# Retention and squared-ReLU feed-forward on one core: every engine's tasks in a new written order, and other places for the long 64x64 runs

## The chip, the cores and the metric

The kernel runs on 1 core of one Trainium2 chip. The metric is device microseconds of one execution; of several runs the median counts. Three runs of the kernel before gave 284.87, 284.90 and 284.92 us.

## The reference

```python
# q, k, v: 8 batches x 8 heads x 576 positions x 64, f32
scores = q @ k.T / sqrt(64)                      # per batch and head
ret    = (scores * gamma_h ** (i - j) for i >= j, else 0) @ v
x      = ret with heads side by side             # 4608 tokens x 512
h      = x @ w_in                                # 512 x 2048
out    = (max(h, 0) ** 2) @ w_out                # 2048 x 512, f32
```

## The kernel before, in words

**Units and groups.** The tokens are cut into 36 units of 128 tokens: 32 "full" ones (one batch, one stretch of 128 positions) and four "tails" that join the last 64 positions of two batches. Two units make a group, so there are 18 groups, g0 to g17. The first eight units (four groups) come in pairs of 256 positions (add_load_pair, add_unit_pair, add_ret_pair); the others one by one (add_load, add_unit, add_ret).

**What a group goes through.** SyncE issues the loads of k, q and v. GpSimd (in the first groups VectorE and ScalarE too) casts them to f16, v times a decay. For the pairs TensorE transposes k and q (task ft, L580) and ScalarE copies the result out (fe, L592); for later units a DMA does it (fx2, L541, tile kqT). Then TensorE computes with 64x64 matmuls, four of which run side by side on the quarters of the array (quad, L501, matmuls at L502): scores, sums of k and v for the running state, and the output of the retention. For the pairs these are the tasks fs, fk, fo1 and fo2. From g4 on one task f0 (L938) emits the output of group g, the scores and the sums of group g+1 in one go: 96 to 128 matmuls of 64x64 in a row, the long 64x64 runs; there are 13 of them. VectorE masks the scores, updates the state and writes x of the group (tile xT: fx at L720 for pairs, L894 for the others; two halves each).

**Feed-forward.** add_ff (L1206) makes eight blocks fb0 to fb7 for a group, each of two tasks j0 and j1 of four matmuls (L1229, tile ph): x times w_in. ScalarE applies the ReLU (fr, L1235) and ScalarE or VectorE the square (fg, L1241, tile gT). For g0 the second product takes 16 tasks fi0 to fi15 for each of its two units s0 and s1 (L1270, tile po): fi0 to fi3 need the first piece of w_out, fi4 to fi7 the second, and so on. From g1 on add_strassen (L1286) does it with seven products of halves of the matrices instead of eight (L1327); this takes sums of gT on VectorE (gS, L1294) and differences of w_out (wT, add_wT, L989, eight tasks i0.h0 to i3.h1 on VectorE). Groups 14 to 16 do the same trick in the first product as well (add_ff1s, L1042).

**Weights.** w_in and w_out come in eight pieces w0 to w7 of 512x512 f32, cast to f16 by the DMA that GpSimd issues (add_weight, L472). w0 to w3 are w_in, w4 to w7 w_out. fb6 and fb7 need w3; wT.i0.h0 and fi0 to fi3 need w4. The load of k for units 4 and 5 waits until w5 has landed (behind, L426).

**What sets the order.** Each piece of work is a task of class Schedule (L78): an engine, a length that the planner assumes, a function that emits its instructions, the tasks that it depends on and the buffers that it takes (eight PSUM banks "ff", load buffers, and so on). emit (L107) plays the tasks forward in time with those lengths. Each time an engine is free, it takes the ready task with the lowest key whose buffers are free; the keys are the 1,828 numbers of PLACES. The order of starts is the order in which the functions are called, and so the order of instructions on every engine, which each engine then follows strictly. 34 tasks "warm" (L411) are matmuls on a zeroed tile, which fill TensorE's first microseconds.

**Places of the runs.** place_runs (L204) goes through TensorE's tasks in order. Ahead of each long run (size over 190 instructions) it takes the next number of PADS and spreads that many no-operations over the small matmul tasks since the run before; sched.filler emits them. PADS moves the run to another place in TensorE's instruction stream and changes nothing else. Before it was

```python
    PADS = (136, 0, 0, 0, 121, 0, 84, 0, 76, 0, 0, 0, 0)      # 417
```

## Time and profile before

| what | value |
|---|---|
| time, median of 3 runs | 284.9 us |
| span of the profiled execution, first to last instruction | 284.5 us |
| what lies around the span (difference of the two) | 0.4 us |
| TensorE matmuls busy | 277.1 us (97%) |
| VectorE, ScalarE, GpSimd busy | 195.8, 190.6, 87.3 us |
| granted TensorE clock | 1.000 |
| moved by DMA | 50.0 MB, mean 176 GB/s |
| TensorE's instructions fetched (instruction queue) | 37 packets, 0.61 MB |

The span counts from the first to the last instruction of the program; all times below are from its start. Busy times of TensorE overstate its work, since matmuls are pipelined: a matmul of 256 columns is listed with 273 ns, but one starts every 109 ns. So the distance from one start to the next is what a matmul costs on TensorE, and every longer distance is a wait or a change of form. By engine "PEld" the profile lists the weight loads, which run beside the matmuls. SP is SyncE's queue.

### The profile page before, as it was taken

The page shows a single profiled execution, that of the slowest core. Times are in us where ns is not written, and L with a number is a line of the kernel's source. Part 1 is how long each engine was busy: PE and PEld are TensorE (multiplying, and loading weights), DVE is VectorE, ACT ScalarE, POOL GpSimd, SP SyncE. Part 2 cuts the span into 40 slices and gives each one's busy share as a digit, 9 for nine tenths or more (in the row PEclk, how much of TensorE's full clock was granted, in tenths as well). Part 3 has the DMA queues.
Part 4 walks back from the last instruction along what each step waited for, and adds up shares of the span by engine and source line. Part 5 has one row for each costly group of instructions (what it writes and reads, how often), then busy time and mean ns, then how long its engine had stood idle before and what let it go on. Part 6 is the DMA issues. An engine that isn't in the chain of part 4 may idle for free.

```text
span 284.5 us, 10916 instructions
## 1 busy us (share of the span) xinstructions
PE 277.1 (97%) x4490; PEld 237.7 (84%) x4490; DVE 195.8 (69%) x371; ACT 190.6 (67%) x360; POOL 87.3 (31%) x123
## 2 busy tenths in 40 slices
PE   8899999999999999899999999999999999999994
PEld 3578767888888888788888888888988999899883
DVE  4783489756867769635859485866986889765742
ACT  5659884678495848566575767577657486668830
POOL 6550035445334346434342523353243200000000
PEclk9999999999999999999999999999999999999999
DMA  7999998999997989999989969999998902020205
GB/s 204 291 207 205 261 313 233 155 241 167 197 189 165 225 193 177 195 241 198 234 196 215 208 163 198 200 146 249 200 168 215 193 0 78 2 76 1 76 0 150
DMA packets 119152, 50.00 MB, mean 176 GB/s; under 512 B 94784, under 2 KB 113728, under 8 KB 119104
## 3 DMA queue, kind: packets, MB, share of 16 engines
q1 hardware_dynamic: 114560, 44.84, 73.4%
q0 software_dynamic: 4224, 4.19, 8.9%
q8 instruction: 37, 0.61, 0.9%
q10 hardware_dynamic: 320, 0.26, 0.3%
q14 instruction: 11, 0.09, 0.1%
HBM read 36.70 MB, written 9.44 MB: 162 GB/s over the span
## 4 chain that ended last, share of the span: by engine, by line
PE 84%; DMA 11%; SPq 3%; POOL 1%; issue 0%; DVE 0%; POOLq 0%
PE po L1327 36%; PE ph L1229 31%; PE ph L1072 7%; DMA w_out<-in_moe_w_out_dram 6%; PE psO L502 4%; DMA pair<-in_v_dram 2%; PE po L1270 2%; PE psc L502 2%; PE psS L502 2%; DMA kqT<-kq 2%; SPq L460 1%; DMA loads<-in_v_dram 1%; SPq L463 1%; PE psT L584 1%; POOL w_out L478 1%; SPq L543 0%
## 5 line engine op out<-in xcount | busy, mean ns | idle before, releaser
L1229 PE MATMUL ph<-xT,w_in 128*128 128x256 f16 x960 | 117.4, 273 | 0.0
L1229 PEld LDWEIGHTS <-w_in 128*128 128x128 f16 x960 | 93.3, 98 | 11.8
L1237 ACT ACTIVATE rl<-ph 128x512 f16<-128x512 f32 x120 | 70.4, 590 | 42.3 <-PE ph L1229 41.7
L1247 ACT ACTIVATE gT<-rl 128x512 f16<-128x512 f16 x101 | 63.4, 630 | 2.7
L1327 PEld LDWEIGHTS <-gS 128*128 128x128 f16 x544 | 51.6, 98 | 6.1
L1327 PE MATMUL po<-wT,gS 128*128 128x256 f16 x408 | 54.9, 273 | 0.0
L1327 PEld LDWEIGHTS <-gT 128*128 128x128 f16 x408 | 39.5, 98 | 4.8
L1300 DVE TENSOR_TENSOR gS<-gT,gS 128x512 f16<-128x512 f16 (+1 forms) x51 | 32.3, 640 | 9.9 <-ACT gT L1247 9.2
L532 POOL TENSOR_TENSOR v<-loads,vdec_full 128x512 f16<-128x512 f32 x24 | 27.2, 1133 | 36.1 <-DMA loads<-in_v_dram 33.0
L1327 PE MATMUL po<-w_out,gT 128*128 128x256 f16 x272 | 37.6, 273 | 0.0
L1300 DVE TENSOR_TENSOR gS<-gT 128x1024 f16<-128x1024 f16 x34 | 25.7, 760 | 11.8 <-ACT gT L1247 9.0
L516 POOL CAST kq<-loads 128x512 f16<-128x512 f32 x32 | 22.1, 692 | 34.7 <-DMA loads<-in_k_dram 26.9
L1350 DVE TENSOR_TENSOR o<-po,u 128x256 f32<-128x256 f32 x33 | 13.9, 422 | 22.7 <-PE po L1327 14.6
L527 POOL CAST kq<-loads 128x512 f16<-128x512 f32 x24 | 16.8, 700 | 31.0 <-DMA loads<-in_q_dram 31.0
L1340 ACT COPY u<-po 128x256 f32<-128x256 f32 x34 | 12.4, 368 | 16.6 <-PE po L1327 16.4
L898 DVE TENSOR_TENSOR xT<-psO,gam_full 128x512 f16<-128x512 f32 x28 | 18.6, 683 | 5.8 <-PE psO L502 5.7
L1327 PE MATMUL po<-wT,gT 128*128 128x256 f16 x136 | 18.8, 273 | 0.0
L1327 PE MATMUL po<-w_out,gS 128*128 128x256 f16 x136 | 18.6, 273 | 0.0
L838 DVE TENSOR_TENSOR rT<-psc,mask_full 128x512 f16<-128x512 f32 x24 | 15.7, 681 | 0.6 <-PE psc L502 0.6
L1106 DVE CUSTOM_DVE_ANT_0 gT<-ph,loads 128x512 f16<-128x512 f32 x18 | 12.1, 685 | 4.2 <-PE ph L1072 3.5
L611 DVE TENSOR_TENSOR R<-stmp,dec 128x512 f16<-128x512 f32 (+1 forms) x18 | 13.5, 750 | 0.4
L1350 DVE TENSOR_TENSOR o<-po,p 128x256 f32<-128x256 f32 x18 | 7.6, 422 | 7.2 <-issue 3.5
(101 smaller groups left out, 310.3 us busy)
## 6 DMA issues: line engine op xcount, KB each, us to landing
out_dram<-o SPq DMA_DIRECT2D x32, 256.0 KB, 2.8
loads<-in_k_dram SPq DMA_DIRECT2D x24, 256.0 KB, 4.6
loads<-in_q_dram SPq DMA_DIRECT2D x96, 64.0 KB, 3.1
loads<-in_v_dram SPq DMA_DIRECT2D x24, 256.0 KB, 3.8
w_in<-in_moe_w_in_dram POOLq DMA_DIRECT2D x4, 512.0 KB, 8.9
w_out<-in_moe_w_out_dram POOLq DMA_DIRECT2D x4, 512.0 KB, 14.4
pair_c<-in_k_dram SPq DMA_DIRECT2D x2, 512.0 KB
pair_c<-in_q_dram SPq DMA_DIRECT2D x4, 256.0 KB
```

The lines of the kernel that those rows point to most:

```text
L502: t = nc.tensor.matmul(out_, lhsT=lhsT, rhs=rhs, start=start, stop=True, skip_group_check=True, tile_position=(64 * row, 64 * col))
L516: op(out=out_.rearrange("p (n b a d) -> p n b a d", n=2, b=2, a=2), in_=in_.rearrange("p (a n b) d -> p n b a d", n=2, a=2))
L527: nc.gpsimd.tensor_copy(out=tile_of["kq", u][:, 1].rearrange("p (t a d) -> p a t d", t=4, a=2), in_=tile_of["q32", u].rearrange("p (a t) d ...
L532: nc.gpsimd.tensor_tensor(out=t, in0=tile_of["v32", u], in1=vdec[kind].rearrange("p (h o) -> p h o", o=1).to_broadcast([P, H, D]), op=ALU. ...
L898: nc.vector.tensor_tensor(out=tile_of["x", g].rearrange("p n (s e i) -> p e (n s) i", s=n, e=2)[:, c], in0=y.rearrange("p (o t r) -> p o r ...
L1072: nc.tensor.matmul(out_[:, e], lhsT=left[:, m, fi * P:(fi + 1) * P], rhs=right()[:, m], start=fresh and e == 0 and m == 0, stop=m == HK - ...
L1229: nc.tensor.matmul(tile_of["ph", g, fb][:, j, :], lhsT=w_in16[:, m, fi * P:(fi + 1) * P], rhs=tile_of["x", g][:, m, :], start=(m == 0), st ...
L1237: nc.scalar.activation(out=t, in_=tile_of["ph", g, fb], func=ACTF.Relu)
L1247: nc.scalar.activation(out=t, in_=rl, func=ACTF.Square)
L1300: (nc.gpsimd if eng == "POOL" else nc.vector).tensor_tensor(out=tile_of["S", g][:, k, sl], in0=in0(sl), in1=in1(sl), op=op)
L1327: nc.tensor.matmul(tile_of["pb", g, bank], lhsT=left(i), rhs=right[:, i, :], start=(start and i == 0), stop=(i == HF - 1), skip_group_chec ...
L1350: nc.vector.tensor_tensor(out=o_tile(u)[:, half * HM:(half + 1) * HM], in0=bank(x), in1=tile_of[name, g], op=ALU.add)
```

## The change

The planner's loop in emit and PLACES are gone. In their place stands ORDER, the numbers of all 1,828 tasks in the order in which they are to be emitted. Tasks, lengths, dependences, buffers and the code that each task emits are the same. 359 of TensorE's 863 tasks, 191 of VectorE's 341, 145 of ScalarE's 354, 77 of SyncE's 170 and 29 of GpSimd's 100 stand at another place of their engine, none of them by more than 26. PADS has other numbers, which add 674 no-operations where there were 417, and they may stand after the 58th task of TensorE (FIRST_PAD), where it was a planned start later than 24.0 us.

```diff
-PLACES = """
-1001794 1001795 1001796 1001797 1001798 1001799 1001800 1001801 1001802 ...
+ORDER = """
+0 34 1 2 3 35 4 5 6 36 7 8 9 70 10 71 11 37 12 76 72 13 73 77 14 38 78 15 ...
...
     def emit(self):
-        assert len(PLACES) == len(self.tasks)
-        for t, x in zip(self.tasks, PLACES):
-            t["key"] = int(x)
-        ready = {e: [] for e in self.LAT}
...
-        assert len(order) == len(self.tasks)
+        order = [self.tasks[int(x)] for x in ORDER]
+        assert len(order) == len(self.tasks) == len(set(ORDER))
+        for t in order:
+            assert t["left"] == 0, t["n"]
+            for w in t["users"]:
+                w["left"] -= 1
         self.place_runs([t for t in order if t["eng"] == "PE"])
         for t in order:
             t["fn"]()
             for i in range(t["pad"]):
                 self.filler()
...
-    PADS = (136, 0, 0, 0, 121, 0, 84, 0, 76, 0, 0, 0, 0)
+    PADS = (121, 55, 15, 0, 38, 23, 79, 3, 67, 71, 147, 55, 0)
+    FIRST_PAD = 58
...
-        for t in tasks:
+        for i, t in enumerate(tasks):
...
-            elif t["size"] <= 8 and t["key"] < 10 ** 6 and t["start"] > 24.0:
+            elif t["size"] <= 8 and i >= self.FIRST_PAD:
                 between.append(t)
```

The two orders around the first pieces of w_out, task by task (numbers are places among TensorE's tasks, counted from 0; the first 58 are the same tasks in both):

```
TensorE  before: 58 g1.fb0.j0  59 g0.fb6.j0  60 g0.fb6.j1  61 g0.fb7.j0  62 g0.fb7.j1  63 g1.fb0.j1  64 g1.fb1.j0  65 g0.fi0.s0
TensorE  after:  58 g0.fi0.s0  59 g0.fb6.j0  60 g1.fb0.j0  61 g1.fb0.j1  62 g0.fb6.j1  63 g0.fb7.j0  64 g0.fb7.j1  65 g0.fi1.s0
VectorE  before: xT g1 first half, xT g1 second half, wT.i0.h0
VectorE  after:  xT g1 first half, wT.i0.h0, xT g1 second half
```

Further on, the transposes of q of units 4 and 5 (ft) stand at place 93 where they stood at 108, and VectorE's cast of v of units 4 and 5 stands ahead of ten tasks (both halves of wT.i1, wT.i2.h1, both halves of wT.i3, three sums gS, a square and a step of the state); in the order before, it stood behind all ten. The long runs f0 of g4, g5, g6 and g7 stand at places 208, 252, 297 and 357, where they stood at 209, 251, 303 and 338; the later ones moved by two places at most. The last 44 tasks of TensorE and the order of the final stores on ScalarE are the same.

## The prediction

> **What bounds the kernel now.** I read the page first, then TensorE's timeline, then what the other engines waited for.

> ```profile
> span 284.5 us, 10916 instructions
> PE 277.1 (97%) x4490; PEld 237.7 (84%) x4490; DVE 195.8 (69%) x371; ACT 190.6 (67%) x360; POOL 87.3 (31%) x123
> DMA   7999998999997989999989969999998902020205
> ```

> TensorE is busy in 97% of the span, and DMA in nine tenths or more of most slices up to about 228 us. TensorE is the bound, with DMA close behind. Going by starts in TensorE's timeline (109 ns from one 256-column matmul to the next), I find almost no gap after 17.4 us. From there to the end only two waits are left: 0.22 us ahead of g0.fi8 (a piece of w_out that landed at 32.50) and 1.3 us inside the run f0 of g7. So an order can gain little; what it can lose is set by what TensorE's tasks wait for. In the front that is the weights. VectorE's timeline shows when pieces of w_out land:

> ```profile
> start us, us, engine line op out<-in xcount [idle before <-releaser]
> 22.43 1.29 DVE L723 TENSOR_TENSOR xT<-psO,gam_full 128x512 f16<-128x512 f32 x2 [1.78 <-PE psO L502]
> 26.68 0.69 DVE L994 TENSOR_TENSOR wT<-w_out 128x1024 f16<-128x1024 f16 x1 [2.96 <-DMA w_out<-in_moe_w_out_dram]
> ...
> 29.23 0.69 DVE L994 TENSOR_TENSOR wT<-w_out 128x1024 f16<-128x1024 f16 x1 [1.35 <-DMA w_out<-in_moe_w_out_dram]
> 32.59 0.69 DVE L994 TENSOR_TENSOR wT<-w_out,wT 128x1024 f16<-128x1024 f16 x1 [2.68 <-DMA w_out<-in_moe_w_out_dram]
> ```

> VectorE sat idle three times until a piece had landed: w4 at 26.66, w5 at 29.20, w6 at 32.50 (the trace's landings; w1 to w3 19.03, 21.57, 24.15). A piece takes 2.54 us. TensorE in the same stretch:

> ```profile
> 23.72 3.55 PE L1229 MATMUL ph<-xT,w_in 128*128 128x256 f16 x31
> 27.10 1.03 PE L1270 MATMUL po<-w_out,gT 128*128 128x512 f16 x4
> ...
> 32.54 1.02 PE L1270 MATMUL po<-w_out,gT 128*128 128x512 f16 x4
> ```

> The first four L1270 matmuls, fi0 to fi3 of g0, start at 27.10, 0.44 us after w4's landing; the row at 32.54 starts 0.04 us after w6's. The old order leads TensorE just behind the weights.

> **The change, part by part.**

> *First product with w_out.* The first 58 TensorE tasks are the same in both orders and ended at 24.05. The new order has g0.fi0 next, which needs w4. SyncE's first 20 tasks and GpSimd's first 15 are in the same order, so w4 lands at 26.66 as before. TensorE does nothing from 24.05 to 26.71 (0.05 for the release): **+2.66**. All of TensorE is queued behind it, and nothing hides it. If the front runs up to 0.3 earlier, the wait is that much longer.

> *xT of g1 behind wT.* VectorE now has wT.i0.h0, which needs w4, between the two halves of xT of g1. It starts at 26.68, and two such operations in a row take 1.29 (the pair at 22.43), so the second half is there at 27.97. TensorE does fi0 (0.22) and g0.fb6.j0 (0.44) up to 27.37; g1.fb0.j0 needs both halves and starts at 28.02: **+0.65**. The old order had done the same work at 24.05 + 0.66 = 24.71; the delay is 3.31.

> *What this delay covers.* fi8 comes at 35.64, long after w6: the old 0.22 goes, **-0.22**. The transposes of q of units 4 and 5, 15 places earlier now, would have come at 36.23 and come at 36.23 + 3.09 = 39.32. GpSimd's casts for them, which wait for the load, end at 39.15:

> ```profile
> 37.98 1.17 POOL L567 CAST qx<-pair_c 128x512 f16<-128x512 f32 x2 [19.66 <-DMA pair_c<-in_q_dram]
> 39.76 1.17 POOL L562 TENSOR_TENSOR vx<-pair_c,vdec_pair 128x512 f16<-128x512 f32 x1 [0.61 <-DMA pair_c<-in_v_dram]
> ```

> That is just enough, and it means that the delay at this place could hardly be under 2.9 even if w4 came sooner. VectorE's cast of v waits for the same load as the second row (39.6) with ten tasks behind it. At 0.42 to 0.69 each I get wT.i2.h1 at 42.4, wT.i1.h0 at 43.0, the last sum at 45.4; TensorE asks for them at 45.4, 46.9 and after 50. The four masks of g2 then end near 49.1, and fo1 of g2 comes at 49.2. So it costs nothing by 0.1 us; I take **+0.1**, between 0 and 0.5.

> *The run of g7.*

> ```profile
> 115.30 0.30 PE L502 MATMUL psc<-kqT 64*64 64x64 f16 x16
> 116.71 0.32 PE L502 MATMUL psc<-kqT 64*64 64x64 f16 x16 [1.11 <-DMA kqT<-kq]
> ```

> Inside this run TensorE waited 1.3 us (from 115.41 to 116.71, 0.03 of it usual) for a transposing DMA. In the new order f0 of g7 has 19 tasks (4.2 us) more ahead of it, and the delay adds 3: it comes near 122. SyncE's queue has that DMA at the same place, 72 (it is limited by earlier DMAs, not by TensorE), so the wait goes: **-1.27**. What is late next is the 109 ns pace of TensorE itself.

> *Places of the runs.* The page's instruction queue fetched 9,436 TensorE instructions in 37 packets, so 256 in each. By starts, the thirteen runs take 1.22 to 1.45 us with 128 matmuls, 1.19 to 1.32 with 112, 0.89 and 0.98 with 96 (without the wait above). Over the best of each kind that is 1.2 us in all, in short stops of 0.05 to 0.15 mostly. Counted in the stream modulo 512, the runs that begin at 25 to 69 lose 0.14, 0.13, 0.05, 0.08, 0, 0.13 and 0.15 (mean 0.10); those at 491 to 511 nothing; those at 307 to 393 0.23, 0.20 and 0.09. The new numbers put eleven of the thirteen at 47 to 56, next to the first kind. Thirteen times 0.10 is 1.3 against 1.2 now: **0**, between -1.2 (all at their best) and +1.2 (all as slow as the slowest of their kind).

> *No-operations.* 257 more. Tasks of four matmuls with four of them take 0.437 us, like those with none, so they hide under the matmuls. Fifteen tasks now get 5 to 9, which no row shows: 0 if they hide, and if twelve instructions in 0.437 us were already the limit, 5 more of 0.036 in twelve tasks, +2.2. Nearest is the row with four: **0**.

> *Rest.* For every pair of TensorE task and the ScalarE or VectorE result that it needs, I compared the TensorE work in between. By kind, the least is nearly the same in both orders (0.89 instead of 1.09 us at ScalarE copies of 0.59). The end of the stream is the same.

> **Sum:** +2.66 + 0.65 - 0.22 + 0.1 - 1.27 + 0 + 0 = +1.92 on a span of 284.5 with 0.4 around it, that is on the median 284.9: **286.8 us**.

> [...]

> **Rivals.**

> *A: the weights are not late.* Faster than before. The new order fits a w4 that lands by 24.0 (and a q that comes as much sooner, since the load of k ahead of it waits for w5): then +2.66 and +0.65 vanish and 284.9 - 0.22 - 1.27 = 283.4 is left. The loss in front is landing minus 23.35, so it decides at a landing of 24.84, 1.8 us sooner than the trace's. For it speaks only how consistently the order is laid out for early loads; against it, the three idle rows above. Pieces would have to take 2.2 instead of 2.54 us. Chance 0.10.

> *B: the runs at their best.* 286.8 - 1.2, without the +0.1 and with pieces of 2.50 instead of 2.54 (five of them, -0.2): 285.3 to 285.5, no difference that counts. Against it: three of four old runs at 69 did stop. Chance 0.06.

> *C: TensorE slows down after the idle stretch.*

> ```profile
> 1.25 4.99 PE L411 MATMUL warm<-wT 128*128 128x512 f16 x12 [1.25 <-DVE wT L292]
> ```

> The first eleven matmuls start every 427 ns, from 5.9 us on every 216: 4.6 us at half pace cost 2.3. If the idle stretch brings that back: 289.1. Against it: after the 1.3 us at 115.41 the next matmuls keep 109 ns. Chance 0.04. [...]

> *D: the order isn't what the lists say.* Excluded as far as the built program goes: its streams show ORDER's sequence, with the weights' semaphore on fi0 and on wT.i0.h0.

> **Chances.** The forecast's case (285.5 to 288.6) has 0.80, A 0.10, B 0.06, C 0.04. The range goes from B's low end, 285.3, to 286.8 + 1.2 + 0.5, about 288.5, and 0.1 for the rounding; the no-operations' full price fits in only if the runs gain. It leaves out A and C. A measurement of this kernel tells 0.2% (0.6 us) from no change. Faster by more: 0.10 (A). Within: 0.06 (B). Slower: 0.84.

> **What would show it.** In the profile after: TensorE idle from about 24.05 to 26.7 ahead of an L1270-like matmul, released by w_out's DMA, and again until 28.0 ahead of ph, released by xT; wT at 26.7 between the xT halves; no wait in a run near 122; long runs of 1.2 to 1.45 us. A first fi0 before 26 would prove me wrong, and so would 256-column matmuls further apart than 110 ns after 28 us (C) or around the fifteen tasks ahead of f0 of g14 (no-operations).

## The result and the profile after

The changed kernel takes **297.5 us** where the kernel before takes 284.9: ratio 1.0454, 95% interval 1.0432 to 1.0477, that is 12.6 us more. The forecast was 286.8 and its range ended at 288.6. Times are medians; one execution of b_padsA below, of 293.6 us, was in a slower state of the chip and is left out of its median.

The head of its page, to be read against the three lines of before:

```profile
span 295.5 us, 11176 instructions
PE 283.0 (96%) x4490; PEld 236.0 (80%) x4490; DVE 192.7 (65%) x371; ACT 186.1 (63%) x360; POOL 88.6 (30%) x123
DMA  6999998989899999977998778779997602010104
```

The span is 11.0 us longer, the number of matmuls is the same, and VectorE and ScalarE are busy for less time. So TensorE lost the 11 us in stops and in matmuls that start at longer distances, not in more work. To find them I went through the starts of all matmuls in both traces and added up what each distance has beyond the usual one of its form (109 ns for 256 columns, about 10 ns for a 64x64 matmul in a long run). The sums by stretch, in us:

| stretch | before | after | what is in it after |
|---|---|---|---|
| to 20 us | 12.58 | 12.82 | the start and the matmuls called warm, in both |
| 20 to 50 | 2.16 | 5.24 | the stop ahead of fi0, then matmuls at 0.21 us |
| 50 to 100 | 1.32 | 3.00 | a few waits of 0.1 to 0.3 |
| 100 to 180 | 2.62 | 2.49 | before: 1.30 in f0 of g7; after: 1.33 in f0 of g6 |
| 180 to 200 | 0.52 | 0.92 | a wait for VectorE |
| 200 to 220 | 0.42 | 4.37 | tasks with 4 to 9 no-operations |
| 220 to the last matmul | 0.98 | 1.89 | waits for VectorE, 0.9 |
| behind the last matmul's start | 3.96 | 4.78 | the last stores |

The front came as forecast, with one thing more. VectorE's timeline:

```profile
22.68 0.69 DVE L639 TENSOR_TENSOR xT<-psO,gam_full 128x512 f16<-128x512 f32 x1 [2.05 <-PE psO L418]
27.00 0.69 DVE L910 TENSOR_TENSOR wT<-w_out 128x1024 f16<-128x1024 f16 x1 [3.62 <-DMA w_out<-in_moe_w_out_dram]
27.60 0.68 DVE L639 TENSOR_TENSOR xT<-psO,gam_full 128x512 f16<-128x512 f32 x1
```

TensorE's timeline in the same stretch:

```profile
22.54 1.92 PE L1145 MATMUL ph<-xT,w_in 128*128 128x256 f16 x16
27.11 0.59 PE L1186 MATMUL po<-w_out,gT 128*128 128x512 f16 x1 [2.64 <-DMA w_out<-in_moe_w_out_dram]
27.48 4.03 PE L1145 MATMUL ph<-xT,w_in 128*128 128x256 f16 x24
```

The half of xT stands behind wT, and fi0 waits for w_out, as the prediction says. But the one matmul of fi0 takes 0.59 instead of 0.38 us, and the 24 matmuls behind it 4.03 instead of 2.8. The busy times by stretch say why; the column behind POOL is the granted TensorE clock:

```profile
core 0: us, PE busy (x) PEld busy (x) DVE busy (x) ACT busy (x) POOL busy (x), PEclk, DMA share, GB/s
22.00:24.00 2.00, 1.91 (x38) 1.51 (x27) 0.69 (x1) 1.48 (x4) 0.00 (x0) 1.00 1.24 206
24.00:27.00 3.00, 0.46 (x5) 0.17 (x2) 0.01 (x1) 2.84 (x6) 0.00 (x0) 0.94 1.24 205
27.00:30.00 3.00, 2.89 (x13) 1.81 (x14) 1.29 (x2) 0.00 (x0) 0.00 (x0) 0.50 1.24 206
30.00:36.00 6.00, 6.00 (x50) 4.67 (x48) 0.88 (x2) 4.79 (x9) 0.00 (x0) 1.00 1.17 284
```

From 27 to 30 us the clock was half. Thirteen matmuls start 0.1 us late each, 1.4 us in all. That is rival C, to which I gave 0.04.

Three more losses were in no rival (a fourth, of 0.8 us at the last stores, comes below). First, the inside of f0 of g6, by TensorE's timeline:

```profile
106.05 0.38 PE L418 MATMUL psS<-v,kq 64*64 64x64 f16 x24
107.58 0.26 PE L418 MATMUL psS<-v,kq 64*64 64x64 f16 x8 [1.15 <-issue]
```

TensorE stood still for 1.33 us in the middle of the sums, behind the 72nd of 128 matmuls, and nothing that the profile shows released it ("issue"). Second, the tasks ahead of f0 of g14, where 20 matmuls of 256 columns take 3.11 us:

```profile
206.74 0.38 PE L1243 MATMUL po<-wT,gT 128*128 128x256 f16 x2
207.17 3.11 PE L1145 MATMUL ph<-xT,w_in 128*128 128x256 f16 x20
210.43 0.38 PE L1243 MATMUL po<-wT,gT 128*128 128x256 f16 x2 [0.15 <-issue]
```

The tasks of four matmuls with 8 no-operations (eight of them) last 0.586 to 0.739 us from start to start, those with 9 (four) 0.658 to 0.748; all those with 0 to 4 have a median of 0.437. Third, VectorE's results come too late. VectorE's timeline, then GpSimd's, then TensorE's, where the second row waited:

```profile
182.74 1.15 DVE L1165 TENSOR_TENSOR gT<-rl 128x512 f16<-128x512 f16 x1
183.81 0.68 DVE L754 TENSOR_TENSOR rT<-psc,mask_full 128x512 f16<-128x512 f32 x1
184.41 0.41 DVE L1216 TENSOR_TENSOR gS<-gT,gS 128x512 f16<-128x512 f16 x1
```

```profile
182.57 1.04 POOL L448 TENSOR_TENSOR v<-loads,vdec_full 128x512 f16<-128x512 f32 x1 [3.35 <-DMA loads<-in_v_dram]
```

```profile
183.29 1.25 PE L1243 MATMUL po<-wT,gS 128*128 128x256 f16 x10
184.88 0.61 PE L1243 MATMUL po<-wT,gS 128*128 128x256 f16 x4 [0.33 <-DVE gS L1216]
```

The square at 182.74 (gT<-rl) took 1.15 us beside GpSimd's cast of v. In VectorE's timeline of before, with GpSimd idle, it took 0.41:

```profile
176.26 0.41 DVE L1249 TENSOR_TENSOR gT<-rl 128x512 f16<-128x512 f16 x1
```

This is no single case: in the seventeen traces this operation takes 0.41 to 0.43 us all 219 times that no cast or product of GpSimd runs beside it, and 0.41 to 1.30 the 104 times that one does. The new order also puts a mask of g12 ahead of the sum gS that TensorE asks for next. Such waits cost 0.49 us here and 0.13 to 0.40 at 171, 201 and 231 to 235 us.

### The profile page after: what moved, and what is told of

Same layout as the page of the kernel before. It is cut to its first block, busy times and chain, and to the rows that moved or that the text cites. A ratio compares the mean times of both kernels' runs of the same rounds, so it can differ in the third digit from the quotient of the medians.

```text
span 295.5 us, 11176 instructions
## 1 busy us (share of the span) xinstructions
PE 283.0 (96%) x4490; PEld 236.0 (80%) x4490; DVE 192.7 (65%) x371; ACT 186.1 (63%) x360; POOL 88.6 (30%) x123
## 4 chain that ended last, share of the span: by engine, by line
PE 88%; DMA 4%; DVE 3%; issue 1%; ACT 1%; POOL 1%; DVEq 0%
PE po L1243 35%; PE ph L1145 34%; PE ph L988 6%; DMA w_out<-in_moe_w_out_dram 4%; PE psO L418 4%; PE warm L327 3%; PE po L1186 2%; PE psc L418 2%; PE psS L418 2%; PE psT L500 1%; DVE gS L1216 1%; DVE gT L1165 1%; DVE rT L754 0%; ACT rl L1153 0%; ACT gT L1163 0%
## 5 line engine op out<-in xcount | busy, mean ns | idle before, releaser
L1145 PE MATMUL ph<-xT,w_in 128*128 128x256 f16 x960 | 121.9, 274 | 0.6
L1163 ACT ACTIVATE gT<-rl 128x512 f16<-128x512 f16 x101 | 62.2, 631 | 1.4
L1243 PE MATMUL po<-wT,gS 128*128 128x256 f16 x408 | 56.6, 273 | 0.4 <-DVE gS L1216 0.3
L432 POOL CAST kq<-loads 128x512 f16<-128x512 f32 x32 | 23.5, 734 | 69.1 <-DMA loads<-in_k_dram 53.2
L1243 PEld LDWEIGHTS <-gT 128*128 128x128 f16 x408 | 38.5, 98 | 6.9 <-issue 2.1
L1216 DVE TENSOR_TENSOR gS<-gT 128x1024 f16<-128x1024 f16 x34 | 27.3, 804 | 17.8 <-ACT gT L1163 14.1
L1243 PE MATMUL po<-w_out,gT 128*128 128x256 f16 x272 | 38.6, 273 | 0.0
L1216 DVE TENSOR_TENSOR gS<-gT,gS 128x512 f16<-128x512 f16 (+1 forms) x51 | 30.8, 606 | 10.5 <-ACT gT L1163 10.0
L1266 DVE TENSOR_TENSOR o<-po,u 128x256 f32<-128x256 f32 x33 | 13.9, 420 | 20.8 <-PE po L1243 11.8
L443 POOL CAST kq<-loads 128x512 f16<-128x512 f32 x24 | 16.6, 693 | 20.6 <-DMA loads<-in_q_dram 20.6
L1165 DVE TENSOR_TENSOR gT<-rl 128x512 f16<-128x512 f16 x19 | 9.0, 476 | 15.3 <-ACT rl L1153 15.1
L327 PE MATMUL warm<-wT 128*128 128x512 f16 x34 | 11.4, 465 | 1.3 <-DVE wT L208 1.3
```

What stands on the lines that cost most here:

```text
L327: nc.tensor.matmul(warm_ps[0], lhsT=junk[:, 0:P], rhs=junk, start=True, stop=True)
L432: op(out=out_.rearrange("p (n b a d) -> p n b a d", n=2, b=2, a=2), in_=in_.rearrange("p (a n b) d -> p n b a d", n=2, a=2))
L443: nc.gpsimd.tensor_copy(out=tile_of["kq", u][:, 1].rearrange("p (t a d) -> p a t d", t=4, a=2), in_=tile_of["q32", u].rearrange("p (a t) d ...
L1145: nc.tensor.matmul(tile_of["ph", g, fb][:, j, :], lhsT=w_in16[:, m, fi * P:(fi + 1) * P], rhs=tile_of["x", g][:, m, :], start=(m == 0), st ...
L1163: nc.scalar.activation(out=t, in_=rl, func=ACTF.Square)
L1216: (nc.gpsimd if eng == "POOL" else nc.vector).tensor_tensor(out=tile_of["S", g][:, k, sl], in0=in0(sl), in1=in1(sl), op=op)
```

## The experiments

Every time is compared with the kernel before on the same chip; "above" means above it. The kernels called a_ are the changed kernel with an edit, those called b_ the kernel before with one.

### The front

a_front:

```diff
 TensorE  g0.fb5.j1
-TensorE  g0.fi0.s0
 TensorE  g0.fb6.j0 g1.fb0.j0 g1.fb0.j1 g0.fb6.j1 g0.fb7.j0 g0.fb7.j1
+TensorE  g0.fi0.s0
-VectorE  xT g1 first half, wT.i0.h0, xT g1 second half
+VectorE  xT g1 first half, xT g1 second half, wT.i0.h0
```

> The changed kernel with two tasks moved: TensorE's g0.fi0.s0 goes six places back, behind g0.fb7.j1, and VectorE's wT.i0.h0 goes behind both halves of xT of g1. Theory: the stop ahead of fi0 (2.8 us) and the half granted clock behind it (thirteen matmuls at 213 instead of 109 ns, 1.4 us) are one thing and go together, 4.2 us less: 293.3 us, granted clock 1.00 from 24 to 30 us. Rival, the cover of my prediction: the transposes of q of units 4 and 5 at place 93 then come before GpSimd's casts (end 39.15) and wait some 2.8 us there, so that only the clock's 1.4 us comes back: 296.1 us.

Measured: 295.9 us, ratio 1.0387 (1.0342 to 1.0432), 11.2 us above. The stop ahead of fi0 is gone and the clock is 1.00 throughout, but TensorE's timeline has a new stop:

```profile
35.83 0.81 PE L1186 MATMUL po<-w_out,gT 128*128 128x512 f16 x3
38.78 0.40 PE L500 MATMUL psT<-ident,qx 128*128 128x128 f16 x4 [2.13 <-POOL qx L483]
39.33 0.40 PE L500 MATMUL psT<-ident,qx 128*128 128x128 f16 x4 [0.16 <-POOL qx L483]
```

The transposes of q of units 4 and 5 wait for GpSimd's casts. That is what the prediction says of the cover: at place 93 they can't do with less delay. The rival holds; only the clock's part came back.

a_front2 puts these transposes and VectorE's start back as well:

```diff
-TensorE  transposes of q, units 4 and 5, at place 93
+TensorE  transposes of q, units 4 and 5, behind g0.fi12.s1
+VectorE  first 54 tasks in the order before
```

> The changed kernel with its front put back fully: g0.fi0.s0 behind g0.fb7.j1, the transposes of q of units 4 and 5 behind g0.fi12.s1 (they stood at place 93), and VectorE's first 54 tasks in the order before. Theory: without the stop at fi0 the early transposes were the next to wait (2.3 us); with both moved, nothing in front waits, the clock stays whole, and 4 to 4.5 us of the 12.6 come back: 8 to 8.6 us above the kernel before. Rival: a third place of the new front waits as well, and more than 10 us are left.

Measured: 294.1 us, ratio 1.0328 (1.0313 to 1.0344), 9.2 us above. So 3.4 of the 12.6 us went. It lies between the two expectations: the stretch from 20 to 40 us loses 0.6 us (the kernel before 0.8), but two waits of 0.40 and 0.98 us appear at 46 and 48 us, for VectorE's rx (masked scores) and for GpSimd's cast of v of the next units, and two of 0.78 and 0.71 us at 114 and 187 us, for VectorE's Rm (the state) and gS. That the order of the other engines was made for the late front would explain it, but no run shows that.

b_fi0_58 and b_fi0_59 move one task of the kernel before:

```diff
 TensorE  g0.fb5.j0 g0.fb5.j1
+TensorE  g0.fi0.s0
 TensorE  g1.fb0.j0
 TensorE  g0.fb6.j0 ... g1.fb1.j0
-TensorE  g0.fi0.s0
```

and the same with g0.fi0.s0 behind g1.fb0.j0.

> The kernel before with one task moved: g0.fi0.s0 from place 65 to 58 of TensorE. Theory: 2.7 us of idle TensorE until w4 has landed and then half the granted clock for some 3 us, 1.4 us more: 288.4 to 288.9 us, mean granted clock 0.994. Rival, as in the prediction's sum: the idle time alone, clock 1.00: 287.2 us.

> The kernel before with g0.fi0.s0 moved from place 65 to 59, one task of 0.44 us later than in the kernel above. Theory of a limit between the 2.3 us that left the clock whole in the changed kernel with its front moved back, and the 2.8 us that halved it: 2.2 us idle, clock 1.00, 286.8 us. Rival, a limit below 2.2 us: 288.0 to 288.4 us and half the clock behind the idle time.

Measured: 288.7 us, ratio 1.0120 (1.0065 to 1.0175), 3.0 us above, and 287.2 us, ratio 1.0090 (1.0053 to 1.0128), 1.6 us above. In the first the trace shows 3.06 us of idle time and the half clock. The second tells most, because its executions differ: those with a mean granted clock of 0.998 to 1.000 have spans of 285.0 to 285.4 us, those with 0.993 287.2 to 288.0. The half clock costs some 2 us by itself. The profile caught one of the latter. TensorE's timeline and the stretches:

```profile
23.28 1.36 PE L1145 MATMUL ph<-xT,w_in 128*128 128x256 f16 x11
26.83 0.38 PE L1186 MATMUL po<-w_out,gT 128*128 128x512 f16 x1 [2.18 <-DMA w_out<-in_moe_w_out_dram]
```

```profile
24.00:27.00 3.00, 0.82 (x7) 0.50 (x6) 0.28 (x1) 1.75 (x3) 0.00 (x0) 1.00 1.24 207
27.00:30.00 3.00, 3.00 (x17) 2.08 (x16) 0.41 (x1) 1.23 (x2) 0.00 (x0) 0.56 1.24 206
```

Here a stop of 2.35 us (between starts, less one matmul) was enough. But the length of the stop does not decide. In a_sp below, the longest of all, 3.32 us at the same spot, left the clock whole. TensorE's timeline and three stretches:

```profile
26.84 0.38 PE L1186 MATMUL po<-w_out,gT 128*128 128x512 f16 x1 [3.15 <-DMA w_out<-in_moe_w_out_dram]
```

```profile
22.14:25.55 3.41, 1.55 (x15) 1.14 (x12) 0.46 (x1) 2.89 (x7) 0.00 (x0) 1.00 1.25 207
25.55:28.96 3.41, 1.70 (x13) 1.21 (x14) 1.29 (x2) 0.51 (x1) 0.00 (x0) 1.00 1.24 206
28.96:32.38 3.42, 3.42 (x32) 2.87 (x30) 0.00 (x0) 2.31 (x4) 0.00 (x0) 1.00 1.24 207
```

And in a_others, also below, a stop of 1.88 us inside f0 of g6 halved it:

```profile
104.72:108.13 3.41, 1.71 (x132) 1.44 (x131) 0.43 (x1) 0.85 (x2) 0.00 (x0) 1.00 0.74 163
108.13:111.54 3.41, 3.41 (x18) 2.43 (x17) 3.38 (x5) 0.50 (x1) 2.90 (x5) 0.50 1.23 125
```

So a fixed length between 2.3 and 2.8 us, as I expected, is refuted.

The traces' records of the granted clock show what went with the half clock. In all seventeen the clock changes only at whole multiples of 3.413 us after its first rise: in the changed kernel it rises at 6.13 us, falls at 26.61, six such stretches later, and rises at 30.03, one later. I cut each trace into these stretches and added up in each the time between the end of a matmul's usual distance and the next start (gaps of over 0.04 us). Of 1,409 stretches at full clock, the 25 with 2.11 us or more of it (8 inside the kernels, 17 behind their last matmuls) were followed by half clock, and the 1,384 with 2.05 or less were not. The changed kernel's has 2.31 us (23.20 to 26.61), that of b_fi0_59 2.35, that of a_others 2.13 with its smaller gaps. The two of a_sp have 2.02 and 1.88, because a boundary cuts its stop. The first rise lies 4.1 to 6.9 us after the span's start, differently from trace to trace. That can let one kernel come out both ways, as b_fi0_59 did, with mean clocks of 0.993 and of 0.998 to 1.000.

### The no-operations

a_noops0 and b_noops147:

```diff
-    PADS = (121, 55, 15, 0, 38, 23, 79, 3, 67, 71, 147, 55, 0)
+    PADS = (121, 55, 15, 0, 38, 23, 79, 3, 67, 71, 0, 55, 0)
```

```diff
-    PADS = (136, 0, 0, 0, 121, 0, 84, 0, 76, 0, 0, 0, 0)
+    PADS = (136, 0, 0, 0, 121, 0, 84, 0, 76, 0, 147, 0, 0)
```

> The changed kernel with the eleventh number of PADS 147 -> 0, so that the tasks between f0 of g13 and f0 of g14 get no no-operations (the runs of g14 to g16 begin 147 instructions earlier). Theory: TensorE takes one instruction in some 36 ns, and beyond four no-operations in a task of four matmuls each costs that: 12 tasks with 8 or 9 and 11 products with 4 or 5 lose 3.2 to 3.6 us together, all of which comes back: 293.9 us. Rival: the no-operations hide and the losses from 206 to 217 us are late inputs or the fetch of instructions: 297.5 us.

> The kernel before with the eleventh number of PADS 0 -> 147: ten tasks of four matmuls ahead of f0 of g14 get 8, two get 9, and twelve products 4 or 5 no-operations. Theory of one instruction in 36 ns: 10 x 0.146 + 2 x 0.182 + 11 x 0.073 + 0.109 = 2.7 us more, up to 3.5 if the fetch of instructions adds to it: 287.6 to 288.4 us. Rival: no-operations hide under matmuls: 284.9 us, within 0.3.

Measured: 295.2 us, ratio 1.0361 (1.0288 to 1.0433), 10.5 us above; and 288.4 us, ratio 1.0127 (1.0097 to 1.0157), 3.7 us above. The second is the clean one: same order, one number. (It moves the later runs too, and its trace has a stop of 0.78 us in f0 of g15, at 222 us, of the kind of the next section; so not all of the 3.7 us is the no-operations' own.) The same 24 matmuls of ph, in TensorE's timeline of the kernel before and of b_noops147:

```profile
201.03 2.78 PE L1229 MATMUL ph<-xT,w_in 128*128 128x256 f16 x24
```

```profile
199.32 3.80 PE L1229 MATMUL ph<-xT,w_in 128*128 128x256 f16 x24
```

The tasks last 0.586 us and more with 8 no-operations, as in the changed kernel. Sixteen instructions in 0.586 us are 37 ns each, the median task has 40. So twelve instructions in 0.437 us, 36 ns each, had been the limit already. In a_noops0 the losses between 200 and 220 us fall from 4.37 to 0.95. Its median fell by only 2.3, but its interval is wide, since its executions differ by the clock of the front: spans of 292.0 and 292.4 us at a mean clock of 0.999 and more, 294.4 and 295.7 at 0.991 and less.

### The stop in f0 of g6

If nothing releases TensorE, its instructions may be missing. The trace has the packets of the instruction queue, 16 KB each, one for 256 instructions (37 packets for 9,436 in the kernel before). In the changed kernel one runs from 104.80 to 106.19, and TensorE goes on at 107.58. I counted instructions in the stream: the stop lies ahead of number 3266, and 3266 modulo 256 is 194. The other stop of this kind, 0.98 us in the sums of the second group at 16.44, is ahead of number 451, which is 195 modulo 256. From 56 us on, the other packets start at most 3.0 us after TensorE has passed the 194th instruction of a block, and end 1.9 us or more before the next 194th. Here it started 5.0 us after, and the run had used up the block.

a_place and a_sp:

```diff
-    PADS = (121, 55, 15, 0, 38, 23, ...
+    PADS = (121, 55, 115, 78, 116, 23, ...
```

```diff
-SyncE, GpSimd  order of the changed kernel
+SyncE, GpSimd  order of the kernel before
```

(The 88th matmul in the first expectation is a miscount; it is the 72nd.)

> The changed kernel with PADS (121, 55, 115, 78, 116, ...) in place of (121, 55, 15, 0, 38, ...): f0 of g6 begins 100 instructions later in TensorE's stream, f0 of g7 178 later, all others where they were modulo 256. Theory: the stop of 1.3 to 2.2 us behind matmul 88 of f0 of g6 is a block of 256 instructions that is fetched too late, because the run begins some 80 instructions after the fetch could begin and uses up the block in 1 us; 100 short instructions more give the fetch 5 us more: no stop inside f0 of g6, 295.6 to 296.2 us. Rival: the last eight matmuls of the sums wait for a cast or a load that is late: the stop stays behind matmul 88, 297.5 us.

> The changed kernel with SyncE's and GpSimd's tasks in the order before throughout; TensorE, VectorE, ScalarE and PADS as changed. Theory: the fetch of instructions before f0 of g6 is late (5 us behind the point that triggers it, elsewhere 2.5 at most) because SyncE has 18 transfers issued without a break from 94.7 to 105 us; in the old order it is not, and the stop in f0 of g6 (1.3 to 2.2 us) goes, with 0.8 us at the last stores: 10 to 10.6 us above the kernel before. Rival: the place of the run makes the fetch late, the stop stays, and only the stores' 0.8 us come back: 11.8 us above.

Measured: 296.3 us, ratio 1.0399 (1.0351 to 1.0448), 10.6 us above; and 295.8 us, ratio 1.0400 (1.0374 to 1.0426), 10.9 us above. In a_place the run has no stop, but 46 instructions behind it, in the middle of an ordinary task, TensorE stops for 1.43 us, again ahead of a 194th instruction:

```profile
108.14 0.38 PE L1145 MATMUL ph<-xT,w_in 128*128 128x256 f16 x2
109.79 0.38 PE L1145 MATMUL ph<-xT,w_in 128*128 128x256 f16 x2 [1.27 <-issue]
```

The packet for it ended at 108.18. A stop that moves with the count of instructions, and not with a matmul or its data, is a late fetch: the rival falls. In a_sp the stop is gone, which spoke for SyncE's transfers as the cause of the delay. The next kernels took that back.

### What comes late from VectorE, and the last stores

a_others and a_tail:

```diff
-VectorE from task 179, ScalarE from 203, GpSimd from 75, SyncE from 137: order of the changed kernel
+VectorE from task 179, ScalarE from 203, GpSimd from 75, SyncE from 137: order of the kernel before
```

```diff
-SyncE  stores of u33, u34, u32, u34, u35, u35
+SyncE  stores of u34, u32, u33, u34, u35, u35
```

> The changed kernel with the tasks of VectorE, ScalarE, GpSimd and SyncE in the order before from about 165 us on (from VectorE's task 179, ScalarE's 203, GpSimd's 75, SyncE's 137); TensorE's order and PADS as changed. Theory: TensorE's waits at 171, 184, 201 and 231 to 235 us (1.5 us in all) come from the order on VectorE and from casts of v on GpSimd that now run beside VectorE's sums, and the last stores cost 0.8 us; all go: 295.2 us. Rival: the waits come from TensorE's own order, and only the last stores' 0.8 us come back: 296.7 us.

> The changed kernel with the last six stores of SyncE's queue in the order before (the 256 KB store of u32 ahead of u33, and one 64 KB store of u34 behind both). Theory: the last store was issued 1.1 us after its result because the queue was still busy with the store of u32; with the old order the span is 0.8 us shorter, and if the 1.4 us that lie around the span more than before come from the same stores, the time is 2.2 us shorter: 295.3 to 296.7 us. Rival: the end is set by the last landing whatever the order: 297.5 us.

Measured: 296.2 us, ratio 1.0372 (1.0324 to 1.0420), 10.5 us above; and 296.7 us, ratio 1.0416 (1.0362 to 1.0470), 12.0 us above. TensorE's waits in a_others:

```profile
engine line waited for: us in total, times, longest us
PE po L1186 <- DMA w_out<-in_moe_w_out_dram: 3.1, 1, 3.1
PE psS L418 <- issue: 2.3, 2, 1.7
PE warm L327 <- DVE wT L208: 1.3, 1, 1.3
PE ph L1145 <- DVE xT L814: 0.2, 1, 0.2
```

Those for VectorE's gS and rT are gone, and one of 0.38 us for xT is new. The theory holds for the waits. Of the last stores, SyncE's queue in the changed kernel and in a_tail:

```profile
288.83 0.33 SPq L927 DMA_DIRECT2D out_dram<-o  x1
289.71 0.54 SPq L932 DMA_DIRECT2D out_dram<-o  x1
290.34 0.78 SPq L927 DMA_DIRECT2D out_dram<-o  x1
291.18 1.93 SPq L932 DMA_DIRECT2D out_dram<-o  x3
```

```profile
287.23 1.27 SPq L927 DMA_DIRECT2D out_dram<-o  x2
288.84 2.21 SPq L932 DMA_DIRECT2D out_dram<-o  x3
```

In the first the store of u32, whose result was ready at 288.06, goes out at 290.34 between the last ones, and they queue behind it: the last is issued at 292.55, 1.1 us after its result. In a_tail it goes out earlier, and the span ends 3.93 us after the last matmul's start instead of 4.78. That is the 0.8 us; the times alone (0.6 us less, with overlapping intervals) would not show it. The other 1.4 us that I had looked for here do not exist: time less span is 1.7 us in every execution of the kernel before, too.

### Order and PADS apart

b_padsA and a_padsB: each order with the other kernel's PADS.

```diff
-    PADS = (136, 0, 0, 0, 121, 0, 84, 0, 76, 0, 0, 0, 0)
+    PADS = (121, 55, 15, 0, 38, 23, 79, 3, 67, 71, 147, 55, 0)
```

(b_padsA; a_padsB is the reverse.)

> The kernel before, its order as it was, with the changed kernel's thirteen PADS. Theory: the no-operations ahead of f0 of g14 cost 3.3 to 3.6 us, and no other place of a run costs more than 0.2: 3.5 us above the kernel before. Rival: the late fetch in f0 of g6 comes with the places, and it is 5 us above.

> The changed kernel with the PADS of the kernel before. 3.4 us of no-operations go. f0 of g6 then begins 55 instructions behind the point where a fetch is triggered, not 110, and uses up the block by itself. Theory: the fetch there is as late as in all kernels of the new order but one (5 us, and 2.5 more until its instructions run), so that the stop in f0 of g6 grows to some 3.5 us: 10.5 to 11.5 us above the kernel before. Rival: the late fetch belongs to the place of the run; the stop is under 1 us, and it is 8 us above.

Measured: 288.6 us, ratio 1.0124 (1.0076 to 1.0172), 3.3 us above; and 292.3 us, ratio 1.0237 (1.0196 to 1.0277), 7.0 us above. So the new order alone costs 7 us, the new PADS alone 3.3, and both together 12.6. Most of the other 2.3 can be the stop in f0 of g6, which appears only with both: b_padsA has none there (but one of 0.59 us in f0 of g9, whose packet started 4.0 us after the 194th instruction), a_padsB has none, where I expected it to grow. The run's stretch in a_padsB and in the changed kernel:

```profile
106.20:107.50 1.30, 1.30 (x130) 1.23 (x130) 0.43 (x1) 0.77 (x2) 0.00 (x0) 1.00 0.51 145
```

```profile
105.50:108.20 2.70, 1.55 (x131) 1.31 (x130) 0.42 (x1) 0.83 (x2) 0.10 (x1) 1.00 0.67 161
```

130 matmuls in 1.30 us, with SyncE's order as changed. My theory that the order of transfers delays the packet falls; the place of the run has a part in it.

### All repairs together

a_fixed:

```diff
+TensorE  g0.fi0.s0 and the transposes of q as in a_front2
+VectorE  first 54 tasks, and those from 179 on, in the order before; ScalarE from 203 on too
+SyncE, GpSimd  order of the kernel before
-    PADS = (121, 55, 15, 0, 38, 23, 79, 3, 67, 71, 147, 55, 0)
+    PADS = (121, 55, 15, 0, 38, 23, 79, 3, 67, 71, 20, 55, 0)
```

and a_fixed2, the same with other PADS:

```diff
-    PADS = (121, 55, 15, 0, 38, 23, 79, 3, 67, 71, 20, 55, 0)
+    PADS = (160, 40, 32, 0, 32, 26, 72, 1, 91, 92, 70, 59, 0)
```

> The changed kernel with all five repairs: the front as in the first kernel of this call, SyncE and GpSimd as in the second, VectorE's first 54 tasks and those from 179 on, and ScalarE's from 203 on, in the order before, and PADS' eleventh number 20 instead of 147. TensorE's order behind the front, and the other places of the runs, stay as changed. Theory: front 4.2, no-operations 3.4, fetch 1.6, late inputs 1.5 and last stores 0.8 are 11.5 of the 12.6 us: 0.5 to 1.5 us above the kernel before. Rival: a cause that I have not seen costs more: over 2 us above.

> The repaired kernel of the call before with other PADS (160, 40, 32, 0, 32, 26, 72, 1, 91, 92, 70, 59, 0): the middle of every long run lies near the point that triggers a fetch, 130 instructions on both sides. Theory: the stops of 1.6 us in f0 of g6 and 1.8 us behind f0 of g14 were late fetches and go; what stays is some 1.8 us of waits for VectorE and GpSimd: 2.0 to 2.5 us above the kernel before. Rival: those stops have another cause: 5.5 us above, as before.

Measured: 290.4 us, ratio 1.0198 (1.0175 to 1.0222), 5.5 us above; and 287.7 us, ratio 1.0077 (1.0047 to 1.0106), 2.4 us above. The first refuted my sum: the stop of 1.59 us in f0 of g6 is there again, with SyncE in the order before, and my own choice of 20 put f0 of g14 just ahead of a 194th instruction, so that the run used up the next block in 1.3 us. TensorE's timeline behind it:

```profile
212.13 0.27 PE L1243 MATMUL po<-wT,gS 128*128 128x256 f16 x1
214.02 1.16 PE L1243 MATMUL po<-wT,gS 128*128 128x256 f16 x9 [1.62 <-issue]
```

a_fixed2 puts the 194th instruction near the middle of every long run and has neither stop. Its 2.4 us were expected: 1.0 of them are waits for VectorE at 46, 180 and 185 us, which the mixture of two orders makes, and 0.4 a late fetch at 192 us.

b_center does the same to the kernel before, PADS (154, 55, 1, 72, 1, 26, 51, 1, 92, 92, 72, 63, 0):

> The kernel before with PADS (154, 55, 1, 72, 1, 26, 51, 1, 92, 92, 72, 63, 0), which put the middle of every long run near the point that triggers a fetch, with no more than four no-operations in a task of four matmuls. Theory: every run still passes one such point and pays 0.1 us there; at most 0.3 us less than the kernel before. Rival: the old places were better, up to 0.5 us more.

Measured: 286.1 us, ratio 1.0038 (1.0007 to 1.0068), 0.8 us above. None of its long runs loses more than 0.3 us, but neither do those of the kernel before, f0 of g7 in the one profile apart; there was nothing to gain. No version found here beats the kernel before.

## Why the prediction was wrong

Point by point, by the trace of after:

| step | forecast | trace | |
|---|---|---|---|
| fi0 waits for w4 | +2.66 | +2.81 | right |
| xT of g1 behind wT | +0.65 | +0.05 | right cause, but TensorE was at half clock and came later itself |
| half clock behind the stop | rival C, 0.04 | +1.4 | wrong |
| fi8 no longer waits | -0.22 | -0.22 | right |
| v, masks and xT of g2 | +0.1 | +0.2 | right |
| stop in f0 of g7 goes | -1.27 | -1.27, but see below | wrong for the median |
| places of the runs | 0 | +1.6 | wrong: 1.33 in g6, 0.25 at 55.85 |
| no-operations | 0 | +3.6 | wrong |
| other results, last stores | 0 | +1.7 and +0.8 | wrong |

The trace column sums to 10.7 of the 11.0 us between the two spans.

**The base.** "That is on the median 284.9" took the profiled execution for a typical one, with 0.4 us around its span. In 45 executions of the kernel before, run beside the experiments, the median span is 283.3 us (282.4 to 285.3), and 1.7 us lie around it. The profiled one, with 284.5, was 1.2 us longer than usual, and its 1.3 us in f0 of g7 are about that: in none of the profiles of b_noops147, b_fi0_58, b_fi0_59, b_padsA and b_center, where f0 of g7 has the same place in the order, does the run wait. So the credit of 1.27 us was most likely for a wait that the median doesn't have, and 11.0 us between two profiles are 12.6 between two medians.

**The no-operations** are the largest term. The step "Nearest is the row with four: 0" failed, and the bound beside it was right for one instruction, 36 ns against 37 at best and 40 in the median, but too low in all, +2.2 against +3.6. A row in which something hides says nothing of how much more would hide. Twelve instructions against 0.437 us of array time was a number to be distrusted, and the bound counted five in each of twelve tasks, not the products of two matmuls, which with four no-operations also last 0.3 instead of 0.22 us.

**The half clock.** Against rival C I set a stop of 1.3 us that did not bring it back. That was no measurement near 2.7 us, and 2.11 us in one stretch were enough. Whether a stop of 2.7 us has so much in one stretch depends on where the boundaries fall, so C should have been a main case, at 1.4 to 2 us. It came in the profiled execution and, by the mean clocks of 0.991 and 0.994, in two of the three others.

**The places.** I took the spread of what the old runs had shown, -1.2 to +1.2, for bounds. The race between a run and a fetch did not keep to them: the run uses up a block in 1.3 us, and packets ended up to 7.2 us after the 194th instruction ahead of them. The old places win it, and the old rows could not show what a lost one costs.

**Rest: 0.** I had compared the work of TensorE between each result's neighbours and called the least "nearly the same". That leaves out what the result itself takes: the square took 1.15 instead of 0.41 us beside GpSimd's cast, and the sum behind it came 0.5 us late. And I wrote "the end of the stream is the same" of TensorE and ScalarE, without following SyncE's last six stores.

What was right is the front: that fi0 is late, by how much, from which row, and that the transposes of q hold the front back even without it, which a_front shows.

**Open.** What makes the packet ahead of f0 of g6 start 4.8 to 5.9 us after the 194th instruction in the changed kernel and in six of its variants, but not in a_sp, a_place, a_padsB and a_fixed2, is not settled: neither SyncE's order alone nor the place alone explains it. Open too is why the one execution of the changed kernel with a mean clock of 0.999 took 297.4 us like the others; it has no profile.

## What to carry to other kernels

Before a profile is used as the base of a sum, see how its span stands to those of other executions: a wait that one execution shows may be no part of the median. An instruction that does nothing was free here only up to twelve instructions in 0.437 us: count all of them against the time of the work that hides them, also where a row seems to say that they are free. If an order is laid out by a model of durations, check first the wait that it can't see, a landing, a fetch or a clock, since on TensorE, busy in 96% of the span, they took 2.81, 1.33 and 1.4 us here.
